# Weight pieces of 576 columns, bonus fills on ScalarE alone, and a list schedule on other durations, in a linear-attention kernel with two gated layers

## Chip, core and metric

The program runs on one core of a Trainium2 chip. The metric is the time of one execution on the device in microseconds (us), as the median of several runs. TensorE (PE) does the matmuls and loads their weights (PEld); VectorE (DVE), ScalarE (ACT) and GpSimd (POOL) do elementwise work; SyncE (SP) issues all DMAs.

## What is computed

A linear recurrence with a decaying state per head, then two feed-forward layers. B, H, S, D are 4, 8, 768, 48; the model width is 384, the two inner widths are 768 and 1536. Cut from the reference:

```python
for t in range(S):
    kt, vt, rt = (k[:, :, t], v[:, :, t], r[:, :, t])
    cur = np.einsum('bhd,bhe->bhde', u[None] * kt, vt)
    y[:, :, t] = np.einsum('bhd,bhde->bhe', rt, state + cur)
    state = w[None, :, :, None] * state + np.einsum('bhd,bhe->bhde', kt, vt)
...
h = np.maximum(np.maximum(x @ w1, x @ w2), x @ w3)      # first layer, float64 weights
x = (h @ w_out).astype(np.float32)
...
g = x @ w_gate                                          # second layer, float64 weights
y = (g * (1.0 / (1.0 + np.exp(-g))) * (x @ w_val) @ w_out).astype(np.float32)
```

r, k, v, w, u are float32. The weights of both layers are float64.

## The kernel before

**Attention.** The 768 steps are cut into six blocks of 128, and a block of one batch entry is a unit (24 units, `n`). A unit scales r and k by powers of the decay (`prep_scores`, L266), multiplies u, k and r for the diagonal (`prep_bonus`, L270 and L271, summed in `bonus`, L280), writes the diagonal for eight heads in eight instructions (`fill`, L286 on DVE or L288 on ACT: the eight are two steps of four), multiplies scores (`scores`, L297), selects them below the diagonal (`select`, L300), and multiplies with v and the state (`apply`, L317 to L326; `outer`, L345).

**Layers.** Every layer product is exact to about float32: operands are split into a high and a low float32r part, and `product` (L384, L385, L386) makes three matmuls of each. The first layer (`m`, `o`) runs for six column blocks `i` between the attention units of the next block; then the second layer (`g`, `oo`) runs for the six blocks. `larger` (L401) and `gate` (L429) on DVE read a layer's PSUM banks; `split_low` (L408) on POOL and `split_lo` (L379) on DVE or POOL make low parts.

**Weights.** Each float64 weight is used six times, but brought in and split once. There are three kinds: `a` (6 tiles of 1152 columns, inner layer 1), `b` (2 tiles, its output), `c` (12 tiles, layer 2). A tile is brought in as pieces of 384 columns, two 32-bit words per weight: 18 + 6 + 36 = 60 pieces. A piece takes ten steps: a fetch (L191, four buffers), a scaling on ACT (`scale`, L196), two or three DVE instructions (`top`: L213, L210, L217), two more (`rest`: L225, L227), two on ACT (`put_hi`, L230; `to_float`, L234), and a product on POOL or DVE (`put_lo`, L238). For `a` and `b` pieces, L210 writes its result into a spare tile (`mid`, a part of `x2[0]`), ahead of L217; for `c` pieces it writes over its own input, behind L217. Blocks of layer 1 need all `a` and `b` tiles in block 0, layer 2 needs all `c` tiles in its block 0; the later blocks need no new weight.

**Order.** `Plan` writes each engine's order ahead of time: a list schedule over steps with a cost per engine, in us, and what each step needs. The order of the matmuls is given by hand (`order`); everything else, and whether DVE, ACT or POOL does a step that may run on several, comes out of the costs. The hardware then runs each engine's list in order, with semaphores.

Of the kernel before, what the change touches and what calls it, by code (L numbers as in the profile page):

```python
# [25 lines left out]
W_LO, W_HI = 0.8, 1.25  # L26

# [125 lines left out]
def rwkv_moe(ctx: ExitStack, tc: tile.TileContext, qk, nat, kn, vn, rn, wcol, wh, uh, wup1, wout1, wup2, out):  # L153
# [31 lines left out]
    nearly = 3 * NF1 + NF1  # L185
    weights, raws, ts = {}, {}, {}
    mid = x2[0].bitcast(U32)[:, 0, 0:384]

    def fetch(k):
        raws[k] = raw_p.tile([128, 384, 2], U32, tag="raw", name=f"raw_{k}", bufs=4)  # L190
        nc.sync.dma_start(out=raws[k].rearrange("p n z -> p (n z)"), in_=jobs[k][2].bitcast(U32))  # L191

    def scale(k):

        ts[k] = raw_p.tile([128, 384], U32, tag="t", name=f"t_{k}")
        nc.scalar.mul(ts[k].bitcast(F32), raws[k][:, :, 1].bitcast(F32), 2.0**-112)  # L196

    def part(k, q):
        key, z, _ = jobs[k]
# [3 lines left out]
        return weights[key][:, q, z]  # L203

    def top(k):

        t, hw = ts[k], raws[k][:, :, 1]

        def middle(o):
            nc.vector.tensor_scalar(out=o, in0=hw, scalar1=0x1FF, scalar2=15,  # L210
                                    op0=ALU.bitwise_and, op1=ALU.logical_shift_left)

        nc.vector.tensor_scalar(out=t, in0=t, scalar1=3, scalar2=0xFFFFF000,  # L213
                                op0=ALU.logical_shift_left, op1=ALU.bitwise_and)
        if k < nearly:
            middle(mid)
        nc.vector.scalar_tensor_tensor(out=t, in0=hw, scalar=0x80000000, in1=t,  # L217
                                       op0=ALU.bitwise_and, op1=ALU.bitwise_or)
        if k >= nearly:
            middle(hw)  # L220

    def rest(k):

        lw, hw = raws[k][:, :, 0], raws[k][:, :, 1]
        nc.vector.scalar_tensor_tensor(out=lw, in0=lw, scalar=17, in1=mid if k < nearly else hw,  # L225
                                       op0=ALU.logical_shift_right, op1=ALU.bitwise_or)
# [192 lines left out]
    def second_phase(_):  # L419
        ph1.close()  # L420
        late["moe2"] = pool(ctx, "moe2", bufs=2)
        late["ps_o"] = pool(ctx, "ps_o", space=PSUM)

# [24 lines left out]
    with tc.manual_schedule():  # L448
# [9 lines left out]
        for k in range(4):  # L458
            fetch(k)
# [85 lines left out]
        def attention_closed(_):  # L545
            att.close()
            late["wp2"] = pool(ctx, "wp2", bufs=4, side="right")
# [43 lines left out]
        both, one = {"dve": 0.6, "pool": 1.25}, {"pool": 1.25}  # L591


        for k, (key, z, _) in enumerate(jobs):
            if k < 4:
                add(("fetch", k), {"none": 0.0}, [], lambda e: None, at=17.5 + 1.1 * k)
            else:
                add(("fetch", k), {"sync": 0.5}, [("lo", k - 4), ("branch",)], lambda e, k=k: fetch(k), lag=3.0)

            room = []  # L600
            if key[0] == "c":
                f = key[1] - 4
                room = [("attention closed",)] if f < 0 else [("m", NB - 1, f, 2)] if f < NF1 else [("o", NB - 1, NK - 1, f - NF1)]
            add(("scale", k), {"act": 0.42}, [("fetch", k)] + ([("hi", k - 2), ("rest", k - 2)] if k > 1 else []),
                lambda e, k=k: scale(k))
            add(("top", k), {"dve": 1.02 if k < nearly else 1.2}, [("scale", k)] + ([("rest", k - 1)] if k else []), lambda e, k=k: top(k))
            add(("rest", k), {"dve": 0.74 if k < nearly else 0.86}, [("top", k)], lambda e, k=k: rest(k))
            add(("hi", k), {"act": 0.42}, [("top", k), ("rest", k)] + room, lambda e, k=k: put_hi(k))
            add(("float", k), {"act": 0.42}, [("rest", k)], lambda e, k=k: to_float(k))
            add(("lo", k), {"pool": 1.14, "dve": 0.5}, [("float", k), ("hi", k)], lambda e, k=k: put_lo(k, engine[e]))  # L610

        def weight(k):
            return [("hi", k), ("lo", k)]
# [3 lines left out]
        for n in range(NB * B):  # L617
# [12 lines left out]
            add(("bonus", n), {"dve": 1.0, "pool": 1.95} if first else {"pool": 1.95}, [("arrived", n)],  # L630
                lambda e, n=n: prep_bonus(n, engine[e]))
            add(("keys", n), {"pool": 0.98}, [("bonus", n)], lambda e, n=n: prep_keys(n), at=9.6)
            pair = {2: 0, 4: 2}.get(n, n - 1 if n > 4 else None)
            add(("s", n), {"pe": 1.25}, [("scaled", n, 0), ("scaled", n, 1)] + bank_free["s", n]
                + ([("select", pair, 0), ("select", pair, 1)] if pair is not None else []), lambda e, n=n: scores(n))
            add(("a0", n), {"dve": 0.5}, [("bonus", n)] + ([("y", two)] if n > 1 else []), lambda e, n=n: bonus(n))
# [167 lines left out]
```

## Time and profile before

| | us |
|---|---|
| three runs | 909.99, 910.24, 912.38 (median 910.24) |
| the profiled execution's own time | 909.89 |
| its span, first to last instruction | 908.2 |
| PE matmuls busy | 865.2 (95%) |
| DVE, ACT, POOL busy | 383.5, 323.4, 365.3 |

Of the page's 40 equal slices of the span (22.7 us each), these rows show the busy tenths:

```profile
PE   7869789999999999999998799999999999999998
DVE  8999973333323322448999941121012012112101
```

How to read it: the share of the whole span hides that the work has stages. PE is at 9 tenths everywhere but in slices 0 to 5 and in 20 to 22; in those slices DVE is at 8 or 9, elsewhere at 1 to 4. Those are the stages in which weights are split: `a` and `b` from about 27 us to 130 us, `c` from about 385 us to 529 us.

### The profile page before, as it was taken

What the parts mean: (1) busy time and instruction counts of PE and PEld (TensorE: products, weight loads), DVE (VectorE), ACT (ScalarE), POOL (GpSimd) and SP (SyncE); (2) the same over time, 40 slices, a digit from 0 to 9 for tenths busy, and PEclk for the clock granted to TensorE, in tenths of its full rate; (3) what the DMA queues carried; (4) which work ended last, traced back from release to release, by engine and by line L of the source; (5) the groups of instructions that cost most, each with busy time, mean ns of one, the idle gap of its engine ahead of it and who ended that gap; (6) DMA issues with size and microseconds to landing.
All of it is one profiled execution on the core that took longest, in us unless ns stands there. A gap on an engine that the chain in (4) does not pass through costs nothing.

```text
span 908.2 us, 12109 instructions
## 1 busy us (share of the span) xinstructions
PE 865.2 (95%) x4754; PEld 703.6 (77%) x4754; DVE 383.5 (42%) x615; ACT 323.4 (36%) x675; POOL 365.3 (40%) x322
## 2 busy tenths in 40 slices
PE   7869789999999999999998799999999999999998
PEld 6647668887887887888876578888888888888886
DVE  8999973333323322448999941121012012112101
ACT  3645644342242333325655542122222113122211
POOL 7575666644546635214444442222221222122221
PEclk8889889999999999999999999999999999999999
DMA  8335432323303302012434300000000000000000
GB/s 264 117 100 184 147 125 67 89 75 94 102 1 93 102 1 93 10 36 70 123 106 122 102 36 1 1 35 1 1 1 35 0 1 35 1 1 35 1 1 35
DMA packets 19323, 55.45 MB, mean 61 GB/s; under 512 B 2400, under 2 KB 3296, under 8 KB 19264
## 3 DMA queue, kind: packets, MB, share of 16 engines
q1 hardware_dynamic: 19264, 54.67, 19.6%
q8 instruction: 37, 0.61, 0.3%
q14 instruction: 22, 0.18, 0.1%
HBM read 48.96 MB, written 4.72 MB: 59 GB/s over the span
## 4 chain that ended last, share of the span: by engine, by line
PE 73%; DVE 17%; issue 3%; ACT 1%; DMA 1%; POOL 0%; DVEq 0%; ACTq 0%; POOLq 0%
PE g L386 9%; PE g L385 9%; PE g L384 9%; PE m L384 7%; PE m L386 6%; PE m L385 6%; PE oo L385 5%; PE oo L386 5%; PE oo L384 5%; DVE t L217 4%; DVE raw L225 3%; DVE t L213 2%; DVE raw L210 2%; PE o L386 2%; PE o L384 2%
## 5 line engine op out<-in xcount | busy, mean ns | idle before, releaser
L408 POOL TENSOR_TENSOR gs<-mm,gs 128x512 fp32r<-128x512 f32 x72 | 93.7, 1302 | 287.0 <-ACT gs L433 286.5
L384 PE MATMUL g<-xhi,w_c 128*128 128x512 f32 x432 | 169.5, 392 | 9.7 <-DVE mm L429 9.3
L429 DVE TENSOR_TENSOR mm<-mm,g 128x512 f32<-128x512 f32 x72 | 49.4, 687 | 300.2 <-PE g L386 299.1
L386 PE MATMUL g<-xhi,w_c 128*128 128x512 f32 x432 | 169.3, 392 | 0.9 <-POOL w_c L238 0.8
L385 PE MATMUL g<-xlo,w_c 128*128 128x512 f32 x432 | 168.7, 391 | 0.0
L384 PE MATMUL m<-xhi,w_a 128*128 128x512 f32 x324 | 133.5, 412 | 4.7 <-DVE h L401 4.7
L386 PE MATMUL m<-xhi,w_a 128*128 128x512 f32 x324 | 129.2, 399 | 2.6 <-DVE w_a L238 2.6
L385 PE MATMUL m<-xlo,w_a 128*128 128x512 f32 x324 | 128.7, 397 | 2.3 <-POOL xlo L379 1.4
L401 DVE TENSOR_TENSOR h<-h,m 128x512 f32<-128x512 f32 x72 | 49.3, 685 | 135.7 <-PE m L386 101.2
L384 PEld LDWEIGHTS g<-xhi,w_c 128*128 128x128 f32 x432 | 81.3, 188 | 29.8 <-DVE mm L429 6.1
L408 POOL TENSOR_TENSOR hs<-h,hs 128x512 fp32r<-128x512 f32 x36 | 54.7, 1519 | 103.3 <-ACT hs L405 103.2
L386 PEld LDWEIGHTS g<-xhi,w_c 128*128 128x128 f32 x432 | 81.4, 188 | 18.8 <-POOL w_c L238 1.9
L385 PEld LDWEIGHTS g<-xlo,w_c 128*128 128x128 f32 x432 | 81.4, 188 | 16.8
L433 ACT CAST gs<-mm 128x512 fp32r<-128x512 f32 x72 | 44.6, 620 | 139.3 <-DVE mm L429 139.3
L426 ACT ACTIVATE mm<-g 128x512 f32<-128x512 f32 x72 | 43.0, 597 | 136.9 <-PE g L386 136.9
L384 PE MATMUL oo<-gs,w_c 128*128 128x512 f32 x216 | 85.8, 397 | 0.7 <-ACT gs L433 0.7
L385 PE MATMUL oo<-gs,w_c 128*128 128x512 f32 x216 | 85.3, 395 | 0.9 <-POOL gs L408 0.9
L386 PE MATMUL oo<-gs,w_c 128*128 128x512 f32 x216 | 85.1, 394 | 0.0
L384 PEld LDWEIGHTS m<-xhi,w_a 128*128 128x128 f32 x324 | 62.2, 192 | 21.1 <-ACT w_b L230 3.3
L386 PEld LDWEIGHTS m<-xhi,w_a 128*128 128x128 f32 x324 | 62.2, 192 | 17.3 <-DVE w_a L238 3.5
L385 PEld LDWEIGHTS m<-xlo,w_a 128*128 128x128 f32 x324 | 62.4, 193 | 14.9 <-POOL xlo L379 1.7
L266 POOL TENSOR_TENSOR qk<-qk,P 112x512 f32<-112x512 f32 x43 | 57.0, 1343 | 26.9 <-DMA qk<-in_qk 26.9
(107 smaller groups left out, 1243.7 us busy)
## 6 DMA issues: line engine op xcount, KB each, us to landing
raw<-in_wup SPq DMA_DIRECT2D x54, 384.0 KB, 3.2
nat<-in_nat SPq DMA_DIRECT2D x22, 576.0 KB, 5.1
qk<-in_qk SPq DMA_DIRECT2D x24, 448.0 KB, 4.4
out<-ob SPq DMA_DIRECT2D x18, 256.0 KB, 2.1
raw<-in_wout SPq DMA_DIRECT2D x6, 384.0 KB, 3.3
xr<-xr SPq DMA_DIRECT2D x10, 96.0 KB, 3.0
kv<-in_nat SPq DMA_DIRECT2D x4, 192.0 KB, 9.5
r<-in_nat SPq DMA_DIRECT2D x2, 192.0 KB, 8.2
```

What stands on the lines that cost most here:

```text
L210: nc.vector.tensor_scalar(out=o, in0=hw, scalar1=0x1FF, scalar2=15, op0=ALU.bitwise_and, op1=ALU.logical_shift_left)
L217: nc.vector.scalar_tensor_tensor(out=t, in0=hw, scalar=0x80000000, in1=t, op0=ALU.bitwise_and, op1=ALU.bitwise_or)
L225: nc.vector.scalar_tensor_tensor(out=lw, in0=lw, scalar=17, in1=mid if k < nearly else hw, op0=ALU.logical_shift_right, op1=ALU.bitwise_or)
L266: eng.tensor_tensor(out=a, in0=a, in1=P[0:112], op=ALU.mult)
L384: nc.tensor.matmul(p, wh_, xh, start=first, stop=False)
L385: nc.tensor.matmul(p, wh_, xl, start=False, stop=False)
L386: nc.tensor.matmul(p, wl_, xh, start=False, stop=last)
L401: nc.vector.tensor_tensor(out=hs[i, f], in0=hs[i, f], in1=banks["m", i, f, j], op=ALU.max)
L408: eng.tensor_tensor(out=g[:, 1], in0=m, in1=g[:, 0].bitcast(F32), op=ALU.subtract)
L426: nc.scalar.activation(out=hs[i, f], in_=banks["g", i, f, 0], func=AF.Silu)
L429: nc.vector.tensor_tensor(out=hs[i, f], in0=hs[i, f], in1=banks["g", i, f, 1], op=ALU.mult)
L433: nc.scalar.copy(hsplit[i, f][:, 0], hs[i, f])
```

## The change

Tiles `a` and `c` are brought in as two pieces of 576 columns (a piece may now end inside a 384-column part), `b` in pieces of 384 as before: 12 + 6 + 24 = 42 pieces, with three buffers. The spare tile `mid` goes: in every piece the second word's middle bits are written in place, behind the instruction that reads it. `rest` is split in `rest` and `power`. The bonus fills of the first four units may no longer run on DVE. Three tiles of `c` (not four) wait in the pool that takes the attention's room, one more in a new pool. Costs in the plan are others throughout; two are shown.

```diff
-    jobs = ([(("a", f), z, wup1[f, :, z * 384:(z + 1) * 384]) for f in range(NF1) for z in range(3)]
-            + [(("b", g), z, wout1[3 * g + z]) for g in range(NF1 // 3) for z in range(3)]
-            + [(("c", f), z, wup2[f, :, z * 384:(z + 1) * 384]) for f in range(NF2) for z in range(3)])
+    jobs = ([(("a", f), z, HALF, wup1[f, :, z:z + HALF]) for f in range(NF1) for z in (0, HALF)]
+            + [(("b", g), 384 * z, 384, wout1[3 * g + z]) for g in range(NF1 // 3) for z in range(3)]
+            + [(("c", f), z, HALF, wup2[f, :, z:z + HALF]) for f in range(NF2) for z in (0, HALF)])
...
-        raws[k] = raw_p.tile([128, 384, 2], U32, tag="raw", name=f"raw_{k}", bufs=4)
+        raws[k] = raw_p.tile([128, HALF, 2], U32, tag="raw", name=f"raw_{k}", bufs=3)
...
-            where = late["wp2"] if key[0] == "c" and key[1] < 4 else wpool
+            where = late["wp3" if key[1] == NF2 - 1 else "wp2"] if key[0] == "c" and not 3 <= key[1] < NF2 - 1 else wpool
...
         nc.vector.tensor_scalar(out=t, in0=t, scalar1=3, scalar2=0xFFFFF000,
                                 op0=ALU.logical_shift_left, op1=ALU.bitwise_and)
-        if k < nearly:
-            middle(mid)
         nc.vector.scalar_tensor_tensor(out=t, in0=hw, scalar=0x80000000, in1=t,
                                        op0=ALU.bitwise_and, op1=ALU.bitwise_or)
-        if k >= nearly:
-            middle(hw)
 
     def rest(k):
...
-        nc.vector.scalar_tensor_tensor(out=lw, in0=lw, scalar=17, in1=mid if k < nearly else hw,
+        lw, hw = words(k)
+        nc.vector.tensor_scalar(out=hw, in0=hw, scalar1=0x1FF, scalar2=15,
+                                op0=ALU.bitwise_and, op1=ALU.logical_shift_left)
+        nc.vector.scalar_tensor_tensor(out=lw, in0=lw, scalar=17, in1=hw,
                                        op0=ALU.logical_shift_right, op1=ALU.bitwise_or)
...
+    def power(k):
+
+        nc.vector.tensor_scalar(out=words(k)[1], in0=ts[k], scalar1=0xFF800000, scalar2=None, op0=ALU.bitwise_and)
...
-            add(("lo", k), {"pool": 1.14, "dve": 0.5}, [("float", k), ("hi", k)], lambda e, k=k: put_lo(k, engine[e]))
+            add(("lo", k), {"pool": 1.7 * wide_, "dve": 0.9 * wide_}, [("float", k), ("power", k), ("hi", k)],
...
-                add(("fill", n, x), {"act": 1.2, "dve": 0.75} if first else {"act": 1.2}, [("a0", n)],
+                add(("fill", n, x), {"act": 1.6}, [("a0", n)],
```

What it moves, at three places. In the changed file DVE's five weight instructions are L213, L215, L221, L223 and L228, the product is L239, the gate L431.

DVE, first layer, one piece of an `a` tile with what stands around it (`t` is the scaled word, `raw` the two words of a piece, `x_0` the spare tile, `h` a block of layer 1). Before:

```order
L213 TENSOR_SCALAR t_708<-t_708 128x384
L210 TENSOR_SCALAR x_0_88<-raw_665 128x384
L217 SCALAR_TENSOR_TENSOR t_708<-raw_665,t_708 128x384
L225 SCALAR_TENSOR_TENSOR raw_665<-raw_665,x_0_88 128x384
L227 TENSOR_SCALAR raw_665<-t_708 128x384
L401 TENSOR_TENSOR h_0_705<-h_0_705,m_0_1_692 128x512
```

and now:

```order
L213 TENSOR_SCALAR t_678<-t_678 128x576
L215 SCALAR_TENSOR_TENSOR t_678<-raw_644,t_678 128x576
L221 TENSOR_SCALAR raw_644<-raw_644 128x576
L223 SCALAR_TENSOR_TENSOR raw_644<-raw_644 128x576
L228 TENSOR_SCALAR raw_644<-t_678 128x576
L402 TENSOR_TENSOR h_0_700<-h_0_700,m_0_1_686 128x512
L239 TENSOR_TENSOR w_a_680<-raw_644 128x576
```

Each of the first four instructions is now followed at once by one that needs it; before, an independent one stood between. Of the 18 products of `a` tiles, DVE did six and POOL twelve; of the 12 now, DVE does two and POOL ten.

DVE, second layer, from the third gate on (`mm` is the gated block). Before:

```order
L429 TENSOR_TENSOR mm_2_4135<-mm_2_4135,g_2_1_4122 128x512
L213 TENSOR_SCALAR t_4158<-t_4158 128x384
L217 SCALAR_TENSOR_TENSOR t_4158<-raw_4113,t_4158 128x384
L210 TENSOR_SCALAR raw_4113<-raw_4113 128x384
L225 SCALAR_TENSOR_TENSOR raw_4113<-raw_4113 128x384
L227 TENSOR_SCALAR raw_4113<-t_4158 128x384
L213 TENSOR_SCALAR t_4181<-t_4181 128x384
```

(a second piece follows, before the fourth gate) and now:

```order
L431 TENSOR_TENSOR mm_2_4016<-mm_2_4016,g_2_1_4001 128x512
L228 TENSOR_SCALAR raw_3974<-t_4014 128x576
L213 TENSOR_SCALAR t_4054<-t_4054 128x576
L215 SCALAR_TENSOR_TENSOR t_4054<-raw_4012,t_4054 128x576
L221 TENSOR_SCALAR raw_4012<-raw_4012 128x576
L223 SCALAR_TENSOR_TENSOR raw_4012<-raw_4012 128x576
L228 TENSOR_SCALAR raw_4012<-t_4054 128x576
L431 TENSOR_TENSOR mm_3_4070<-mm_3_4070,g_3_1_4059 128x512
```

Between the first gate and the end of the last piece, DVE has 22 pieces of 384 before and 15 of 576 now, and eleven gates in both. The chain of five inside a `c` piece is the same.

ACT, the fills of the first units (`am` takes the diagonal, `y` and `u` are matmul results). Before:

```order
L288 ACTIVATE am_222<-aeye,a_0_221 128x128 x4
L288 ACTIVATE am_270<-aeye,a_1_269 128x128 x4
L334 COPY xr_291<-y_254 128x3x128
L357 COPY st_131<-u_282 112x192
L288 ACTIVATE am_315<-aeye,a_2_314 128x128 x4
```

and now:

```order
L289 ACTIVATE am_206<-aeye,a_0_205 128x128 x8
L289 ACTIVATE am_253<-aeye,a_1_252 128x128 x8
L335 COPY xr_301<-y_261 128x3x128
L289 ACTIVATE am_299<-aeye,a_2_298 128x128 x8
```

DVE's twelve fills of units 0 to 2 went to ACT. DVE takes over the bonus products of units 0 and 3, and POOL two of the five scalings that DVE had.

## Rows read from the trace of the kernel before

**Rows 1.** Busy time by stretch: us, PE, PEld, DVE, ACT, POOL busy (instructions), PEclk, DMA, GB/s

```profile
30.00:130.00 100.00, 80.32 (x546) 62.31 (x546) 92.37 (x158) 57.50 (x132) 61.30 (x50) 0.86 0.48 153
442.83:537.00 94.17, 82.06 (x325) 63.27 (x324) 84.46 (x141) 53.25 (x106) 44.20 (x39) 0.95 0.33 95
451.10:528.80 77.70, 67.12 (x270) 51.66 (x269) 72.72 (x122) 42.57 (x86) 35.95 (x32) 0.96 0.35 102
537.00:610.45 73.45, 73.45 (x325) 60.81 (x324) 11.36 (x16) 17.47 (x29) 16.70 (x13) 1.00 0.03 11
```

**Rows 2.** Waits of PE over the whole span: us in total, times, longest us

```profile
PE g L384 <- DVE mm L429: 9.3, 6, 2.4
PE y L326 <- DVE am L300: 8.1, 3, 4.3
PE m L384 <- DVE h L401: 4.7, 3, 3.0
```

**Rows 3.** Stretches, instructions on tile raw alone: us, DVE, ACT, POOL busy

```profile
30.00:130.00 100.00, 64.48 (x102) 25.05 (x47) 19.11 (x17) 0.86 0.48 153
451.10:528.80 77.70, 57.34 (x89) 22.86 (x44) 22.70 (x22) 0.96 0.35 102
```

**Rows 4.** The same stretches, L213 alone: us, DVE busy

```profile
30.00:130.00 100.00, 12.81 (x24) 0.86 0.48 153
451.10:528.80 77.70, 11.48 (x22) 0.96 0.35 102
```

**Rows 5.** First stretch, L238 alone (the product): us, DVE busy, POOL busy

```profile
30.00:130.00 100.00, 6.12 (x6) 19.11 (x17) 0.86 0.48 153
```

**Rows 6.** Groups by shape in 451.1 to 528.8: busy us, mean ns, idle before

```profile
L429 DVE TENSOR_TENSOR mm<-mm,g 128x512 f32<-128x512 f32 x11 | 7.5, 678 | 0.0
L408 POOL TENSOR_TENSOR gs<-mm,gs 128x512 fp32r<-128x512 f32 x10 | 13.5, 1346 | 18.4 <-ACT gs L433 17.9 <-DVE t L213 0.4
```

**Rows 7.** One line's instructions, 384 columns: duration ns min/median/max, first and last start

```profile
L213 DVE TENSOR_SCALAR t<-t x60: 340/353/1472, 30.0 to 524.7; 128x384 uint32<-128x384 uint32 x60
L217 DVE SCALAR_TENSOR_TENSOR t<-raw,t x60: 544/559/1686, 30.5 to 525.6; 128x384 uint32<-128x384 uint32 x60
```

**Rows 8.** The same view, pairs of like instructions at 512 and 384 columns

```profile
L379 DVE TENSOR_TENSOR xlo<-x,xhi x12: 678/696/1821, 435.7 to 828.6; 128x512 fp32r<-128x512 f32 x12
L270 DVE TENSOR_TENSOR r<-kv,r x1: 544/544/544, 23.4 to 23.4; 128x384 f32<-128x384 f32 x1
L408 POOL TENSOR_TENSOR gs<-mm,gs x72: 1278/1287/1721, 452.9 to 899.8; 128x512 fp32r<-128x512 f32 x72
L270 POOL TENSOR_TENSOR nat<-nat x22: 995/1021/1466, 8.8 to 357.6; 128x384 f32<-128x384 f32 x22
```

**Rows 9.** Timeline of DVE, an `a` piece and a `c` piece: start us, us

```profile
41.50 0.55 DVE L217 SCALAR_TENSOR_TENSOR t<-raw,t 128x384 uint32<-128x384 uint32 x1
41.97 0.55 DVE L225 SCALAR_TENSOR_TENSOR raw<-raw,x 128x384 uint32<-128x384 uint32 x1
...
448.65 0.56 DVE L217 SCALAR_TENSOR_TENSOR t<-raw,t 128x384 uint32<-128x384 uint32 x1
449.31 0.88 DVE L210 TENSOR_SCALAR raw<-raw 128x384 uint32<-128x384 uint32 x1
```

**Rows 10.** Timeline of POOL at 33.47 us

```profile
33.47 3.01 POOL L238 TENSOR_TENSOR w_a<-raw 128x384 fp32r<-128x384 f32 x1 [6.56 <-ACT raw L234]
```

**Rows 11.** Timeline of DVE, the first unit's fills and selects

```profile
12.42 3.74 DVE L286 TENSOR_SCALAR am<-aeye,a 128x128 f32<-128x128 f32 x4
16.26 1.34 DVE L300 COPY_PREDICATED am<-mask,s 128x512 f32<-128x512 uint8 x2
```

**Rows 12.** Groups in 8 to 30 us: ACT's fills

```profile
L288 ACT ACTIVATE am<-aeye,a 128x128 f32<-128x128 f32 x17 | 5.4, 390 | 12.9 <-DVE a L280 12.9
```

**Rows 13.** DMA issues: KB each, median us to landing

```profile
raw<-in_wup SPq DMA_DIRECT2D x54, 384.0 KB, 3.2
nat<-in_nat SPq DMA_DIRECT2D x22, 576.0 KB, 5.1
```

More of the change, by code (lines that the diff above doesn't have):

```diff
@@ L234, in to_float @@
         nc.scalar.mul(lw.bitcast(F32), lw, 2.0**-35)
     def put_lo(k, eng):
-        raw = raws.pop(k)
-        eng.tensor_tensor(
-            out=part(k, 1), in0=raw[:, :, 1].bitcast(F32), in1=raw[:, :, 0].bitcast(F32), op=ALU.mult)
+        lw, hw = (x.bitcast(F32) for x in words(k))
+        eng.tensor_tensor(out=part(k, 1), in0=hw, in1=lw, op=ALU.mult)
+        del raws[k], ts[k]
     inp, a0s, ams, sc, ys, ups, xr = {}, {}, {}, {}, {}, {}, {}
@@ L422, in second_phase @@
         late["ps_o"] = pool(ctx, "ps_o", space=PSUM)
+        late["wp3"] = pool(ctx, "wp3", side="right")
     def silu(i, f):
@@ L457, in rwkv_moe @@
             load_unit(n)
-        for k in range(4):
+        for k in range(3):
             fetch(k)
@@ L590, in rwkv_moe @@
         add = plan.add
[L591 to L596, printed above, removed]
+        both, one = {"dve": 0.9, "pool": 1.4}, {"pool": 1.45}
+        TOP, REST, POWER = 1.35, 1.35, 0.5
+        for k, (key, z, n, _) in enumerate(jobs):
+            if k < 3:
+                add(("fetch", k), {"none": 0.0}, [], lambda e: None, at=17.5 + 1.7 * k)
@@ L597, in rwkv_moe @@
             else:
-                add(("fetch", k), {"sync": 0.5}, [("lo", k - 4), ("branch",)], lambda e, k=k: fetch(k), lag=3.0)
+                add(("fetch", k), {"sync": 0.5}, [("lo", k - 3), ("branch",)], lambda e, k=k: fetch(k), lag=3.5)
             room = []
             if key[0] == "c":
[L602 to L605, printed above, removed]
@@ L612, in weight @@
-        def weight(k):
-            return [("hi", k), ("lo", k)]
+                f = key[1] - 3
+                room = [("attention closed",) if f < 0 else ("m", NB - 1, f, 2) if f < NF1
+                        else ("o", NB - 1, NK - 1, f - NF1) if f < NF1 + 2 else ("second phase",)]
+            wide_ = n / HALF
+            cast = {"act": 0.2 + 0.48 * wide_}
+            add(("scale", k), cast, [("fetch", k)] + ([("hi", k - 2), ("power", k - 2)] if k > 1 else []), lambda e, k=k: scale(k))
@@ L616, in rwkv_moe, with weight @@
+        def weight(kind, f, j):
+            if kind == "b":
+                return [("lo", 2 * NF1 + f)]
+            k = 2 * f + (nearly if kind == "c" else 0)
+            return [("lo", k + q) for q in ((0,), (0, 1), (1,))[j]]
         arrive = ((5.5, 7.3), (9.0, 10.6), (11.9, 13.5), (14.8, 16.4))
@@ L642, in rwkv_moe @@
+            add(("y", n), {"pe": 2.6 if first else 2.15}, [("select", n, 0), ("select", n, 1)]
                 + ([("row", n - 1)] if n else []) + ([] if first else [("update", n - B)]), lambda e, n=n: apply(n))
-            add(("row", n), {"act": 0.5}, [("y", n)] + ([("xlo", i - 1, k) for k in range(NK)] if i else []),
+            add(("row", n), {"act": 0.6}, [("y", n)] + ([("xlo", i - 1, k) for k in range(NK)] if i else []),
                 lambda e, n=n: evacuate(n))
-            add(("u", n), {"pe": 0.02 if last else 0.5}, [("y", n), ("keys", n)] + bank_free["u", n]
+            add(("u", n), {"pe": 0.02 if last else 0.6}, [("y", n), ("keys", n)] + bank_free["u", n]
```

86 lines of the change are left out of this document (43 added, 43 removed).

## The prediction, made before the changed kernel had run

> **What bounds the kernel now.** I read the slices first, then the stretches, then PE's waits, then DVE inside the two stages that matter. Over the span PE is busy 95%, but by stretch it is not. In 30 to 130 us PE is busy 80.3 of 100 us at a granted clock of 0.86, and DVE 92.4; in 442.8 to 537.0, the first block of layer 2, PE needs 94.17 us for 325 matmuls, and in the next stretch, for as many of the same, 73.45 us at full clock [rows 1]. So the second weight stage alone loses 94.17 - 73.45 = 20.7 us, and that is the most that any faster splitting of `c` can give there. What PE waits for is a DVE result in all its three largest waits: the gate, the select, the maximum [rows 2]. Those instructions are short; they stand behind weight pieces in DVE's queue. From 130 us to 443 us and from 537 us on PE runs without a gap, so what is won or lost in either stage moves the end by as much.
>
> **A piece on DVE now, second stage.** From the first gate at 451.1 us to the end of the last piece at 528.8 us DVE is busy 72.72 of 77.70 us [rows 1]: it is the bound. Of that 57.34 + 11.48 = 68.8 us are the 22 pieces [rows 3, 4] and 7.5 us eleven gates [rows 6]. With the 4.98 us of idle time this makes 81.3, 3.6 more than the stretch, since neighbouring rows overlap at their ends. So a piece costs 68.8 / 22 = 3.13 of rows, +0.23 idle, -0.16 overlap: 3.20 us. Undisturbed, its five instructions take 3 x 0.353 + 2 x 0.559 = 2.18 us (the one-input form three times, the two-input form twice) [rows 7]. With 0.07 net for gaps that leaves 0.95 us per piece, 20.9 us in all, in which DVE's instructions are stretched; POOL is busy 35.95 us there [rows 1], and a like instruction's longest row is three to four times its median on either engine [rows 7, 10]. I take these 20.9 us as waits of the two engines for each other.
>
> **A wider piece.** Two-input DVE instructions take 678 ns at 512 columns and 544 at 384 [rows 8]: 1.05 ns a column, so +0.20 us for 192 more. One-input ones are not shown at two widths. Their cost is between nothing and the same 0.20; L213 at 353 ns against L217 at 559, with the same fixed part of 559 - 384 x 1.05 = 156 ns, has half the slope, so I take +0.10. A piece of 576 costs 2 x 0.20 + 3 x 0.10 = 0.70 us more, undisturbed. On POOL 1287 against 1021 ns [rows 8] gives 2.08 ns a column: +0.40 us for a product.
>
> **Second stage, after.** 15 pieces of 2.18 + 0.07 + 0.70 = 2.95 make 44.3 us, 22 of 2.25 made 49.5: 5.2 us less. The mutual waits have two bounds. If they go by POOL's time, 15 products of 22.70 / 22 + 0.40 = 1.43 us [rows 3] and 13.5 us of low parts [rows 6] are 35.0 against 36.2 us, and 20.9 us shrink by 0.7. If they go by the number of POOL instructions, 25 against 32, they shrink by 4.6. So the stage gains 5.9 to 9.8 us; I take the middle, **-7.8**.
>
> **First stage.** Here the edit cuts both ways. Removed: six pieces, and four of DVE's six products. Added: columns, and a chain. Today an independent instruction stands between those that need each other, and each starts 41.50 + 0.55 - 41.97 = 0.08 us before the last one's row ends; in a `c` piece, a chain, the next one starts 449.31 - 449.21 = 0.10 us after it [rows 9]. So a piece now costs 2.18 - 5 x 0.08 = 1.78 us undisturbed, and a chained one 2.25. 18 x 2.25 + 12 x 0.70 = 48.9 against 24 x 1.78 = 42.7: +6.2 us. Products on DVE: 6.12 us for six [rows 5], after it two of 1.22: -3.7 us. The rest of the 64.48 + 12.81 - 6.12 = 71.2 us that DVE spends on 24 pieces [rows 3 to 5], less 0.16 of overlap each, is 2.81 - 1.78 = 1.03 us a piece, 24.7 us of mutual waits. By POOL's time they grow: 16 products, ten of them of 1.52 us, are 2.8 us more on 61.3 [rows 1, 5], +1.1. By the number of DVE instructions that meet them, 92 against 126, they shrink by 6.7. Sum: +3.6 to -4.2. I take **+1.5**, nearer the upper end, because of the row at 33.47 us: a POOL product, 1.12 us in the mean, took 3.01 us behind an unbroken run of DVE instructions and got in when the run broke [rows 10]. A chain breaks the run after every instruction, so POOL gets in more often and DVE waits more often.
>
> What the Trainium skill says speaks against this term: in "VectorE: DVE Perf Modes", section "The DRAIN you can't avoid", eight copies took the same time with a semaphore after each as with one after the last. By that a chain is free, and the sum would be 8.5 us lower. Rows 9 disagree (overlap in one form, a gap in the other), so the sum goes by the rows.
>
> **Head.** The first unit's four DVE fills take 3.74 us and the selects start at 16.26 [rows 11]. Eight on ACT, at 5.4 / 17 = 0.32 us each [rows 12], end about 2.6 us after 12.4: the selects could start 1.2 us earlier. Unit 1 may gain the same; nothing may come of it if the bonus products that DVE takes over, or the scalings that POOL takes over, are late in their turn. Between 0 and -2.4 I take **-0.8**. ACT does these fills on its idle time (12.9 us ahead of the 17 there); if it were not free, the selects would be what waits.
>
> **What costs nothing, and its cover.** ACT's three steps per piece are off the path (42.6 of 77.7 us busy). Fetches: three buffers instead of four, 576 KB instead of 384. A transfer of 576 KB lands in 5.1 us, one of 384 in 3.2 [rows 13]. A buffer's round is 5.1, two ACT steps of about 0.52 + 0.16 [rows 3], 2.95 + 1.4 of DVE, 1.43 of POOL: 12.2 us, a third of it 4.1 per piece, against (44.3 + 20 + 7.5) / 15 = 4.8 us at which DVE takes pieces. Covered by 0.7 us; before, it was 8.5 / 4 = 2.1 against 3.2. If landings took over 7.2 us, each further one would cost a third of it per piece, 5 us in all for the 15.
>
> **Sum**: -7.8 + 1.5 - 0.8 = -7.1 us against the profiled execution's 909.89, so 902.8; the median of the runs is 0.35 above that execution, so **903.1 us**.
>
> **Rivals.**
> - *Waits go by time, not by number* (13%): both stages at their upper ends, or one-input instructions at the full slope. -5.9 + 3.6 - 0.8 = -3.1; with the slope's 0.10 more on some instructions about -1.5: 908.5. For it: a wait lasts as long as the instruction waited for, and POOL's total time hardly falls. Against it: some DVE instructions meet no POOL one at all, and fewer ends mean fewer meetings.
> - *Slower* (9%): in the first stage POOL becomes the bound. It takes over four products, 4 x 1.52 = 6.1 us, in a fixed order among scalings and low parts that PE waits for. If these are not hidden, the stage costs 6.2 - 3.7 + 1.1 + 6.1 = +9.7, the second gains its lower 5.9, the head nothing: +3.8, so 914.0. It decides once the first stage loses more than the 8.6 us that the rest gives. For it: POOL is busy 61.3 of 100 us already, and its order is fixed. Against it: its 38.7 us of idle time.
> - *A free chain* (8%): the first stage gains 7.0 instead of losing 1.5, so 894.6 us. This is the page's rule. For it nothing here but that the `a` chain might be filled with other steps' instructions; the order shows few.
> - That the edit does not do what it says is excluded by the order: 22 pieces become 15.
>
> **How the numbers follow.** A measurement of this kernel can tell about 0.3%, 2.7 us, from no change. The forecast (70%) spans 897 to 907.5: all terms' better ends together would give 893.8, and are unlikely together. Faster: 70 + 8 = 78%; the same: 13%; slower: 9%. The range from 897 to 909.5 holds the forecast and the first rival and leaves out the other two, 17%.
>
> **What would show it.** Right: from first gate to last piece about 70 us instead of 77.7; PE's wait for the gate below 5 us; the five weight instructions' rows at about 0.45 and 0.76 us undisturbed; first block of layer 2 at about 86 us; its start within 3 us of 442.8. Wrong: that start later by over 5 us with POOL as PE's releaser in the first stage; ACT's scaling waiting for a fetch in the second; one-input rows at 0.55.

## The result: 1.0% faster, and the profile after

Four runs of the changed kernel took 900.78 to 902.76 us, median **901.88**; the kernel before, beside it, had a median of 910.81. The ratio is 0.9899, 95% interval 0.9881 to 0.9918: faster by 1.0%, 1.2 us below the 903.1 that was forecast and inside its range. The profiled execution took 900.78 us, its span is 899.0.

The sum was right; its terms were not, so the close hit is partly luck. From the two traces, by the start of the first matmul of each kind (us):

| | before | after | difference | forecast |
|---|---|---|---|---|
| first matmul of layer 1 (`m`) | 36.22 | 33.26 | -3.0 | -0.8 |
| from there to the first of layer 2 (`g`) | 406.61 | 409.82 | +3.2 | +1.5 |
| first block of layer 2 | 94.17 | 84.62 | -9.6 | -7.8 |
| from its second block to PE's end | 367.37 | 367.36 | 0.0 | 0 |
| sum | | | -9.3 | -7.1 |

The busy time by stretch in the changed kernel, with the columns of [rows 1] (the first stage, the first block of layer 2, from its first gate to the end of its last piece, the block after):

```profile
30.00:130.00 100.00, 78.23 (x503) 59.30 (x499) 95.42 (x118) 51.94 (x105) 64.85 (x51) 0.88 0.49 154
443.08:527.70 84.62, 77.46 (x325) 61.33 (x324) 74.78 (x94) 48.73 (x77) 40.67 (x30) 0.98 0.32 99
448.40:519.00 70.60, 64.97 (x271) 50.98 (x269) 65.65 (x83) 39.68 (x64) 34.92 (x25) 0.98 0.36 110
527.70:601.15 73.45, 73.45 (x326) 60.81 (x325) 11.38 (x16) 17.47 (x29) 16.70 (x13) 1.00 0.03 11
```

The third line answers to 77.70 us of [rows 1]; about 70 had been forecast. The block of the second line is 11.2 us above the 73.45 of the block after it, where it was 20.7 above. Of the 9.6 us that the block lost, 5.0 are idle time of PE and 4.6 its busy time (82.06 to 77.46 us for as many matmuls, at a mean granted clock of 0.98 of full speed instead of 0.95); no run separates the two. In the first line DVE is busy 95.4 us instead of 92.4, for 40 instructions fewer.

PE's waits over the whole span: us in total, times, longest:

```profile
PE m L385 <- DVE h L402: 5.7, 3, 2.9
PE y L327 <- DVE am L301: 5.5, 6, 2.4
PE g L387 <- POOL w_c L239: 5.3, 4, 2.4
```

The wait for the gate, 9.3 us in [rows 2], is gone from the top (1.5 us, once). In its place PE waits for a weight's low part from POOL: the last step of a piece is now late by itself, not what stood ahead of a gate.

The weight instructions one by one, as in [rows 7] (ns, least, median, most):

```profile
L213 DVE TENSOR_SCALAR t<-t x42: 349/455/1410, 28.0 to 514.0; 128x576 uint32<-128x576 uint32 x36, 128x384 uint32<-128x384 uint32 x6
L215 DVE SCALAR_TENSOR_TENSOR t<-raw,t x42: 557/1458/3150, 28.5 to 515.4; 128x576 uint32<-128x576 uint32 x36, 128x384 uint32<-128x384 uint32 x6
L223 DVE SCALAR_TENSOR_TENSOR raw<-raw x42: 558/760/1710, 29.8 to 517.7; 128x576 uint32<-128x576 uint32 x36, 128x384 uint32<-128x384 uint32 x6
L239 POOL TENSOR_TENSOR w_c<-raw x24: 1147/1150/1749, 398.3 to 519.3; 128x576 fp32r<-128x576 f32 x24
```

455 and 760 ns are the undisturbed durations at 576 columns; 0.45 and 0.76 had been forecast. L215 is the odd one: its median is nearly twice L223's, for the same operation and size. It is the one that is held up most.

DVE's busy time on the same lines in the first stage and from the first gate on, `raw` and then L213 (us, DVE, in the first two rows also ACT and POOL busy):

```profile
30.00:130.00 100.00, 69.05 (x72) 22.02 (x34) 18.35 (x16) 0.88 0.49 154
448.40:519.00 70.60, 49.77 (x58) 20.08 (x29) 20.18 (x15) 0.98 0.36 110
30.00:130.00 100.00, 11.71 (x17) 0.88 0.49 154
448.40:519.00 70.60, 11.24 (x14) 0.98 0.36 110
```

Second stage: 61.0 us for 72 instructions (43 one-input, 29 two-input). Undisturbed they are 43 x 0.455 + 29 x 0.760 = 41.6, so they are stretched by 19.4 us. Before it was 68.8 for 111 [rows 3, 4], 67 x 0.353 + 44 x 0.559 = 48.2 undisturbed, 20.6 stretched. Of the 7.8 us that the rows lost, 6.6 are undisturbed time and 1.2 are mutual waits.

The head, on ACT and on DVE, where [rows 11] had fills of 3.74 us on DVE and the selects at 16.26:

```profile
10.38 2.45 ACT L289 ACTIVATE am<-aeye,a 128x128 f32<-128x128 f32 x8
```
```profile
13.20 1.35 DVE L301 COPY_PREDICATED am<-mask,s 128x512 f32<-128x512 uint8 x2 [1.84 <-PE s L298]
```

The selects start 3.1 us earlier, and no longer wait for a fill but for the scores. Those came later, at 11.9 us instead of 10.1: one of the first unit's two scalings stands on POOL now, the first of these two, and ends at 10.8 us, where both were done on DVE at 9.35 before. From 9.7 us up to the scores PE worked on the tile `spare`; whether they could have started sooner is not shown.

```profile
9.22 3.27 POOL L267 TENSOR_TENSOR qk<-qk,P 112x512 f32<-112x512 f32 x2
```

The same row, by a window that ends between the two:

```profile
9.22 1.59 POOL L267 TENSOR_TENSOR qk<-qk,P 112x512 f32<-112x512 f32 x1
```

### The profile page after: what moved, and what is told of

The parts are those of the page before. It is cut to its first block, busy times and chain, and to the rows that moved or that the text cites. A ratio compares the mean times of both kernels' runs of the same rounds, so it can differ in the third digit from the quotient of the medians.

```text
span 899.0 us, 11874 instructions
## 1 busy us (share of the span) xinstructions
PE 858.1 (95%) x4774; PEld 698.3 (78%) x4774; DVE 378.8 (42%) x511; ACT 322.4 (36%) x633; POOL 363.7 (40%) x306
## 3 DMA queue, kind: packets, MB, share of 16 engines
q1 hardware_dynamic: 16672, 54.67, 19.4%
## 4 chain that ended last, share of the span: by engine, by line
PE 76%; DVE 18%; issue 3%; ACT 1%; POOL 1%; DMA 1%; DVEq 0%; POOLq 0%; SPq 0%; ACTq 0%
PE g L387 9%; PE g L385 9%; PE g L386 9%; PE m L385 8%; PE m L387 7%; PE m L386 7%; DVE t L215 5%; PE oo L385 5%; PE oo L386 5%; PE oo L387 5%; DVE raw L221 3%; DVE raw L223 3%; DVE t L213 3%; PE s L298 2%; PE o L387 2%
## 5 line engine op out<-in xcount | busy, mean ns | idle before, releaser
L409 POOL TENSOR_TENSOR gs<-mm,gs 128x512 fp32r<-128x512 f32 x72 | 94.8, 1317 | 277.7 <-ACT gs L435 273.2
L431 DVE TENSOR_TENSOR mm<-mm,g 128x512 f32<-128x512 f32 x72 | 49.5, 687 | 301.3 <-PE g L387 301.3
L409 POOL TENSOR_TENSOR hs<-h,hs 128x512 fp32r<-128x512 f32 x36 | 54.2, 1507 | 90.9 <-ACT hs L406 90.8
L386 PE MATMUL oo<-gs,w_c 128*128 128x512 f32 x216 | 84.6, 392 | 0.1
L385 PE MATMUL oo<-gs,w_c 128*128 128x512 f32 x216 | 84.5, 391 | 0.0
L387 PE MATMUL oo<-gs,w_c 128*128 128x512 f32 x216 | 84.3, 390 | 0.0
L267 POOL TENSOR_TENSOR qk<-qk,P 112x512 f32<-112x512 f32 x45 | 63.2, 1413 | 23.3 <-DMA qk<-in_qk 23.3
```

Source lines behind the costliest of these rows:

```text
L267: eng.tensor_tensor(out=a, in0=a, in1=P[0:112], op=ALU.mult)
L385: nc.tensor.matmul(p, wh_, xh, start=first, stop=False)
L386: nc.tensor.matmul(p, wh_, xl, start=False, stop=False)
L387: nc.tensor.matmul(p, wl_, xh, start=False, stop=last)
L409: eng.tensor_tensor(out=g[:, 1], in0=m, in1=g[:, 0].bitcast(F32), op=ALU.subtract)
L431: nc.vector.tensor_tensor(out=hs[i, f], in0=hs[i, f], in1=banks["g", i, f, 1], op=ALU.mult)
```

## The experiments

All times are medians beside runs of the kernel before on the same chip (910.3 to 911.2 us). Of each trace the table has the start of the first scores, of the first `m`, the time from there to the first `g` (first stage: from 130 us on PE runs without a gap) and the length of the first block of layer 2 (second stage). A trace is one execution, and twelve executions of one kernel, that of the third row, took 904.46 to 910.65 us; so differences of the columns need not add up to those of the medians.

| | time | interval of the ratio | scores | first `m` | to `g` | block |
|---|---|---|---|---|---|---|
| before | 910.4 | | 10.1 | 36.2 | 406.6 | 94.2 |
| fills alone | 908.3 | 0.9963 to 0.9993 | 10.8 | 31.5 | 410.1 | 94.2 |
| 384, spare tile | 908.0 | 0.9964 to 0.9989 | 13.3 | 33.8 | 407.1 | 91.7 |
| 576, spare tile | 898.7 | 0.9842 to 0.9880 | 13.6 | 35.6 | 405.9 | 84.6 |
| the change | 901.9 | 0.9881 to 0.9918 | 11.9 | 33.3 | 409.8 | 84.6 |
| 384, no spare tile | 916.7 | 1.0050 to 1.0087 | 13.3 | 36.2 | 414.9 | 92.4 |
| 576, two spare tiles | 893.6 | 0.9804 to 0.9837 | 13.1 | 35.6 | 404.4 | 80.5 |
| change, products in halves | 897.0 | 0.9834 to 0.9874 | 13.1 | 33.1 | 407.0 | 83.7 |
| change, old head costs | 897.7 | 0.9844 to 0.9874 | 9.9 | 34.1 | 405.9 | 84.7 |
| two spare tiles, products in halves | 891.2 | 0.9775 to 0.9812 | 14.2 | 34.1 | 405.6 | 78.1 |
| two spare tiles, old head costs | 889.2 | 0.9752 to 0.9785 | 10.3 | 34.1 | 403.7 | 79.9 |
| the last + products on DVE | 888.8 | 0.9755 to 0.9786 | 10.5 | 34.6 | 402.5 | 77.5 |
| + low parts in halves as well | 891.9 | 0.9766 to 0.9809 | 10.2 | 34.7 | 406.1 | 80.9 |
| instead: products, low parts in halves | 885.5 | 0.9706 to 0.9744 | 10.7 | 34.4 | 400.8 | 77.4 |

The first five rows are a path from the kernel before to the change. Its steps are the fills; the new durations, together with the split of `rest`; the width, with three buffers instead of four; and the chain. The rows with two spare tiles are the change without its chain, some with one more edit.

**The fills alone.**

```diff
-                add(("fill", n, x), {"act": 1.2, "dve": 0.75} if first else {"act": 1.2}, [("a0", n)],
+                add(("fill", n, x), {"act": 1.2}, [("a0", n)],
```

> The kernel before with one edit: the bonus fills of the first four units may run on ScalarE alone. By the prediction's term for the head: -0.8 us (0 to -2.4), so about 910.0 where the kernel before has 910.8, and the first matmul of layer 1 starts about 0.8 us earlier than 36.22 us. Rival, that the fills alone make the whole of what the changed kernel gained ahead of layer 1: first matmul of layer 1 at about 33.3 us (2.96 us earlier), time about 907.9. Both: the two weight stages as long as before (99.1 and 94.2 us).

908.26 us, 2.1 us faster. Layer 1 begins 4.7 us earlier, more than either text said, but the stage behind it is 3.5 us longer: DVE, which was busy 92.4 of 100 us there [rows 1], still has as many pieces to do. The head and the first stage are not two terms that add up.

**Narrow pieces with the spare tile, all else as changed.**

```diff
-    jobs = ([(("a", f), z, HALF, wup1[f, :, z:z + HALF]) for f in range(NF1) for z in (0, HALF)]
+    jobs = ([(("a", f), z, 384, wup1[f, :, z:z + 384]) for f in range(NF1) for z in (0, 384, 768)]
...
+    mid = x2[0].bitcast(U32).rearrange("p k t -> p (k t)")[:, 0:HALF]
...
+        if k < nearly:
+            nc.vector.tensor_scalar(out=mid[:, 0:jobs[k][2]], in0=hw, scalar1=0x1FF, scalar2=15,
+                                    op0=ALU.bitwise_and, op1=ALU.logical_shift_left)
```

> The changed kernel, with pieces of 384 columns and four buffers, and with the spare tile for the a and b pieces, as before; what is left of the change is the fills, the split of the middle step in two, and the new durations. By the prediction, which gave the new durations no term: as the kernel before but for the head, so 0 to -2.4 us, about 910.0. Rival, that the new order is worth something by itself: the first gate, which stood behind pieces, comes 5.3 us after layer 2 begins, as in the changed kernel, instead of 8.3, and about 3 us are gained in the first block of layer 2; time about 905 to 907.

908.01 us: beside the fills alone the new durations are worth nothing that can be measured. Yet the rival was right about the place. The first gate comes 6.6 us after layer 2 begins (8.3 before, 5.3 after), and the block is 2.5 us shorter. The head is longer, with the first scores at 13.3 us and the first `m` 2.3 us later than with the fills alone; the first stage is 3.0 us shorter. In sum that trace gained 3.2 us, but it is of an execution of 905.46 us, 2.6 below the median; where the median loses the gain again is not shown.

**Wide pieces with the spare tile.** The change with the spare tile's lines from above, for `a` and `b` pieces.

> The changed kernel, with the spare tile again for the a and b pieces, now 576 columns, so that an independent instruction stands between those that need each other; nothing else differs but what the plan makes of it. A free chain (the rival of the prediction): no change, 901.9. A chain that costs its gaps alone (four of 0.035 + 0.08 us in 18 pieces, 8.3 us of DVE): the first stage, 102.3 us from the first matmul of layer 1 to that of its second block, 3 to 8 us shorter, time 894 to 899, and DVE's instructions are stretched as before, 0.37 us each in the mean beyond their undisturbed time. A chain whose every gap lets POOL in ahead of DVE: the stretch falls to the 0.20 us of the kernel before as well, 90 x 0.17 = 15 us more of DVE's time, and the first stage is shorter by more than 8 us, as far as PE lets it.

898.72 us, 3.2 us less than the change. The first stage is 3.9 us shorter, behind a head that is 2.4 longer; as with the fills, the two may trade. Where the head is the same (the first `m` at 34.1 us in both runs with the old head costs, below), the chain is worth 2.2 us of the first stage. DVE in an `a` piece of the change (start us, us), each instruction starting 0.03 to 0.04 us after the last one's row has ended:

```profile
40.89 0.46 DVE L213 TENSOR_SCALAR t<-t 128x576 uint32<-128x576 uint32 x1
41.38 1.74 DVE L215 SCALAR_TENSOR_TENSOR t<-raw,t 128x576 uint32<-128x576 uint32 x1
```

and with the spare tile, each starting 0.08 us before:

```profile
42.44 0.45 DVE L214 TENSOR_SCALAR t<-t 128x576 uint32<-128x576 uint32 x1
42.81 0.45 DVE L217 TENSOR_SCALAR x<-raw 128x576 uint32<-128x576 uint32 x1
43.18 1.70 DVE L219 SCALAR_TENSOR_TENSOR t<-raw,t 128x576 uint32<-128x576 uint32 x1
```

A chain is not free. Its gaps are four of about 0.115 us in a piece, 8.3 us in 18 pieces, and less than half of that reaches the end. It costs no more than its gaps at this width: the time by which DVE's instructions are stretched (table below) stays at 31 to 32 us. That a gap lets POOL in, on which the forecast's +1.5 rested, falls. In an unbroken run the third instruction is held up as long (1.70 us).

**A second spare tile, for `c`.**

```diff
             late["wp2"] = pool(ctx, "wp2", bufs=3, side="right")
+            mids[True] = late["wp2"].tile([128, HALF], U32, name="mid", bufs=1)
```

> As the run before it, and a second spare tile, in the room that attention leaves, for the c pieces too. In the second stage a chain costs 3 x 0.115 + 0.19 = 0.53 us per piece by its gaps, 7.7 us for 14.4 pieces after the first gate. A free chain: no change there. Gaps alone: the first block of layer 2, 84.6 us now, takes about 77. Gaps that let POOL in: the mean stretch of a DVE weight instruction there, 0.24 us (28.4 us for 120), falls towards 0.14, so 12 us more of DVE's time, and the block comes down to what PE needs, 73.5 us: 11 us less than the changed kernel in this stage alone. Time of the kernel: 901.9 less what the spare tile gives in the first stage, and less 0, 7.5 or 11.

893.61 us. Its first block of layer 2, with the columns of [rows 1]:

```profile
440.05:520.53 80.48, 75.39 (x326) 60.27 (x324) 70.88 (x93) 47.94 (x77) 42.81 (x29) 1.00 0.33 104
```

80.5 us, 4.1 less than the change has, and 3.9 us of DVE's busy time less. About half of the 7.7 us of gaps reaches the end; the stretch does not fall here either. With the old head costs in both, the two spare tiles give 8.6 us (897.73 to 889.16), here 8.3.

**Narrow pieces in a chain:** all of the change but the width.

> The changed kernel with pieces of 384 columns and four buffers, without a spare tile: all of the change but the width. The prediction's prices (a chain costs 0.47 us of a piece, 24 pieces; 7 more pieces after the first gate at 2.25, 15 at 0.70 less): first stage 24 x 0.47 = 11.3 us longer than with narrow pieces and a spare tile (99.6), second stage 7.0 longer than the changed kernel's 84.6; time about 915. If a broken chain costs its gaps alone, measured at 3.9 us for 18 pieces, it costs 5.2 for 24: first stage 104.8, second 91.6, time about 912. If the width is worth more where the chain is broken: over 915.

916.67 us, slower than before by 0.7%. The same stretch here:

```profile
451.11:543.46 92.35, 78.21 (x325) 59.27 (x324) 85.31 (x144) 54.47 (x106) 41.98 (x38) 1.00 0.34 99
```
The width is worth 14.8 us to the change, and carries it: without it, the rest of the change loses 6 us. With the spare tile it is worth 9.3 (908.01 to 898.72), so the third text's number came, but not its reason. The chain costs the first stage 7.8 us in 24 pieces, 0.32 us each, where the forecast had 0.47 and the gaps alone, as the text took them from the run before, 0.22. The difference is not explained: 2.0 us more of stretch (table below) are part of it, and the trace with the spare tile is of an execution 2.6 us below its median. In the second stage, with a chain in both, 384 against 576 columns is 92.4 against 84.6.

**Products in halves**, first in the change, then with both spare tiles.

```diff
-        eng.tensor_tensor(out=part(k, 1), in0=hw, in1=lw, op=ALU.mult)
+        o, n = part(k, 1), jobs[k][2] // 2
+        for c in (slice(0, n), slice(n, 2 * n)):
+            eng.tensor_tensor(out=o[:, c], in0=hw[:, c], in1=lw[:, c], op=ALU.mult)
```

> The changed kernel, with every product of a piece written as two instructions of half the columns, on whichever engine does it. In the changed kernel DVE's weight instructions are stretched by 60.6 us in both stages, and POOL's elementwise rows there are 95 and sum to 128 us, the products 39 of them with 48.8 us. From 1148 ns at 576 columns and 827 at 384, a product costs about 0.19 us more in two halves, 7.6 us of POOL's time for 40. If DVE waits by POOL's time (60.6 of 128, 0.47): 3.6 us more of DVE's time, kernel at 902 to 906. If it waits by the number of POOL's instructions (95 become 134): 25 us more, 912 to 927. If a DVE instruction waits for the rest of the one POOL instruction that it meets, so that a shorter one holds it up less and the second half is not met again: the products' share of the wait, about 23 us, falls towards a half, 890 to 897.

> The run with both spare tiles (893.6 us), and the products in halves. By POOL's time: 0 to 4 us slower, 894 to 898. By the number of instructions: over 903. By the length of the instruction that is met: 882 to 889; the unbroken runs of DVE leave POOL's second half to wait, so it could be worth less here than in the kernel with chains.

897.04 us, 4.8 faster, and 891.17 us, 2.4 faster: both between the texts' cases. The intervals of the second and of its kernel with whole products overlap (0.9775 to 0.9812, 0.9804 to 0.9837), so it is not clear of noise alone. In the change, half a product takes (ns, least, median, most):

```profile
L241 POOL TENSOR_TENSOR w_c<-raw x48: 661/837/1261, 395.3 to 514.9; 128x288 fp32r<-128x288 f32 x48
```

That waits go by the number of POOL's instructions is excluded; POOL has 40 more and DVE waits 5.4 us less. That they go by POOL's time is too: its rows in the two stages sum to 146.9 us instead of 128.0. Worked out from the rows, the change has 74 DVE weight instructions that are over 0.1 us longer than undisturbed, 0.81 us in the mean, and with halves there are 94, of 0.58: more meetings, and shorter ones. A shorter instruction holds DVE up less, by far less than half.

**The head's costs**, with both spare tiles and then in the change alone.

```diff
-                add(("scaled", n, q), both if first else one, [("load", n)],
+                add(("scaled", n, q), {"dve": 0.6, "pool": 1.25} if first else one, [("load", n)],
...
-            add(("bonus", n), {"dve": 1.2, "pool": 2.15} if first else {"pool": 2.15}, [("arrived", n)],
+            add(("bonus", n), {"dve": 1.0, "pool": 1.95} if first else {"pool": 2.15}, [("arrived", n)],
```

(and the sums, fills and selects of all units at their old costs).

> The run with both spare tiles (893.6 us), and the costs of the first four units' steps (scalings, bonus products, their sum, fills, selects) as in the kernel before, so that DVE does the first unit's scalings and POOL its bonus product again. If the changed order of the head costs time, as the first scores (13.1 us in that run, 10.8 in the one with the fills alone) and the first matmul of layer 1 (35.6 against 31.5) suggest: 2 to 4 us faster, 890 to 892. If the first stage, bound by DVE, takes back what the head gives, as it did with the fills alone (head 4.7 us shorter, first stage 3.5 longer): within 1.5 us of 893.6.

> The changed kernel, with the costs of the first four units' steps alone as in the kernel before; the fills stay on ScalarE, the chain and the width as in the change. If the new order of the head cost the change what it cost the kernel with both spare tiles (4.5 us): about 897.4. If the head's gain is lost in the first stage where the chain makes DVE's work longer: 900 to 902.

889.16 us, 4.5 faster, and 897.73, 4.2 faster than the change. Here the new costs made a worse order. The gain is not in the head as far as the first `m` (34.1 us instead of 33.3 in the change) but in the first stage, 3.9 us shorter; which of the five costs gives it is not shown. In the trace of the second both scalings of the first unit stand on DVE again:

```profile
7.20 2.14 DVE L267 TENSOR_TENSOR qk<-qk,P 112x512 f32<-112x512 f32 x2
```

They are done at 9.34 us; in the change the one on POOL ended at 10.8. The first scores start at 9.9.

**POOL's work moved or cut**, on the kernel of 889.2 us: products on DVE alone, products and POOL's low parts (L409) in halves, products on DVE and low parts in halves.

```diff
-            add(("lo", k), {"pool": 1.7 * wide_, "dve": 0.9 * wide_}, [("float", k), ("power", k), ("hi", k)],
+            add(("lo", k), {"dve": 0.9 * wide_}, [("float", k), ("power", k), ("hi", k)],
...
-        eng.tensor_tensor(out=g[:, 1], in0=m, in1=g[:, 0].bitcast(F32), op=ALU.subtract)
+        for c in (slice(0, NT // 2), slice(NT // 2, NT)):
+            eng.tensor_tensor(out=g[:, 1, c], in0=m[:, c], in1=g[:, 0, c].bitcast(F32), op=ALU.subtract)
```

> The run with both spare tiles and the old head costs (889.2 us), with every product of a piece on VectorE. DVE does 35 more in both stages, at 0.745 to 0.76 us undisturbed 26 us; POOL loses about 39 rows, 50 of its 130 us. If DVE's waits are a fixed share of POOL's time (61 of 130 us, 0.47): they shrink by 23 us, so no gain and no loss, 887 to 893. If DVE waits about 30 us in each stage whatever POOL does there, as all runs so far show (27 to 34): 26 us more on the engine that bounds both stages, 900 to 915. If PE's waits for POOL's products (5.3 us, 4 times, in the first block of layer 2) go as well: 880 to 886.

> The run with both spare tiles and the old head costs (889.2 us), with products and POOL's low parts of h and gs (512 columns, 1.29 us) in halves. If a shorter POOL instruction holds DVE up less, as with the products alone in the kernel with chains (4.8 us faster) and less with both spare tiles (2.4): 883 to 887. If the fixed part of each more POOL instruction, 0.19 us, outweighs that: 889 to 893; in the later blocks PE has no gap that this could lengthen.

> The run with every product on VectorE (888.8 us), and POOL's low parts of h and gs in halves. If halves help wherever POOL and DVE meet: faster by 1 to 3 us, 886 to 888, still not below the 885.5 of the run with products on POOL in halves. If the gain of that run came from the products' halves alone: 888 to 890.

888.80, **885.49** and 891.93 us. The first is the sharpest look at the mutual waits. Groups from the first gate on (x, busy us, mean ns, idle before and its releaser), with both spare tiles:

```profile
L231 DVE TENSOR_SCALAR raw<-t 128x576 uint32<-128x576 uint32 x15 | 9.6, 639 | 0.0
L214 DVE TENSOR_SCALAR t<-t 128x576 uint32<-128x576 uint32 x14 | 9.2, 658 | 4.1 <-ACT t L202 4.1
L202 ACT ACTIVATE t<-raw 128x576 f32<-128x576 f32 x14 | 10.2, 730 | 6.6 <-DMA raw<-in_wup 6.6
```

and with the products on DVE:

```profile
L242 DVE TENSOR_TENSOR w_c<-raw 128x576 fp32r<-128x576 f32 x15 | 14.3, 951 | 1.3 <-ACT raw L238 1.1
L231 DVE TENSOR_SCALAR raw<-t 128x576 uint32<-128x576 uint32 x16 | 7.2, 451 | 0.0
L214 DVE TENSOR_SCALAR t<-t 128x576 uint32<-128x576 uint32 x15 | 6.8, 452 | 0.3 <-ACT t L202 0.2
L202 ACT ACTIVATE t<-raw 128x576 f32<-128x576 f32 x15 | 11.0, 734 | 15.2 <-DMA raw<-in_wup 12.7 <-DVE mm L434 2.3
```

With POOL's products gone, the one-input rows are at their undisturbed 451 ns. In both stages together DVE does 39 us more (42 products of 40.8 us in sum, instead of two of 1.5), and its waits fall by 33 us (30.3 and 30.7 to 18.8 and 9.2 in the table below). The first case of the text had the time right, but its 23 us of waits were too few. ACT now waits 12.7 us for fetches, but DVE waits for ACT's scaling only 0.2 us, so that costs nothing there; with both spare tiles and products on POOL, DVE stood 4.1 us for that step, which had waited 6.6 us for fetches (L214 and L202 in the first of the two views). A fourth buffer was not tried. Halves (885.49) are the best version of all. The last run, a combination of the two, was a miss: 3.1 us slower by the medians, though the intervals overlap. In its trace PE waited 4.4 us for POOL's low parts in the second stage, 2.7 with them whole; but that execution is 3.3 us above the median, and its mean granted clock is 0.94 from 130 to 160 us, where it is 1.00 with whole low parts. Why halving them helps beside products on POOL and not without them stays open.

**DVE's stretch in all this**, worked out from the rows: for each weight instruction its duration less the undisturbed one (0.353 and 0.555 us at 384 columns, 0.455 and 0.760 at 576), summed from the first `m` to 3 us before the second block's (first stage), and from 385 to 530 us (second); beside it the number of these instructions, and POOL's elementwise rows, which hold POOL's own waits too.

| | DVE, first | POOL, first | DVE, second | POOL, second |
|---|---|---|---|---|
| before | 23.9 us in 106 | 61.8 us in 51 | 31.8 in 180 | 59.1 in 53 |
| fills alone | 23.9 in 106 | 64.1 in 53 | 31.4 in 179 | 60.9 in 54 |
| 384, spare tile | 31.6 in 106 | 70.7 in 57 | 30.5 in 178 | 61.6 in 55 |
| 576, spare tile | 31.4 in 80 | 71.8 in 54 | 28.4 in 119 | 61.4 in 44 |
| the change | 32.2 in 82 | 66.7 in 51 | 28.4 in 120 | 61.3 in 44 |
| 384, no spare tile | 33.6 in 108 | 65.5 in 57 | 29.5 in 173 | 60.4 in 53 |
| change, old head costs | 28.7 in 78 | 65.0 in 49 | 28.5 in 116 | 61.7 in 44 |
| two spare tiles | 29.7 in 80 | 73.1 in 52 | 30.3 in 116 | 65.1 in 45 |
| two spare tiles, old head costs | 30.3 in 76 | 67.8 in 51 | 30.7 in 111 | 62.7 in 46 |
| change, products in halves | 28.3 in 81 | 73.1 in 66 | 26.9 in 117 | 73.8 in 69 |
| products on DVE | 18.8 in 77 | 60.0 in 39 | 9.2 in 110 | 34.3 in 23 |

That these are waits for POOL is seen row by row: in every run each weight instruction that is over 0.1 us longer than undisturbed overlaps a row of POOL (74 of 74 in the change), while of the others most do not (22 of 128 do). DVE's number of instructions (180 against 116) hardly matters; nor does the chain. Taking the products off POOL is what cut the waits most, and halving them cut a little. POOL's sum by itself predicts little: about 65 us of it stand beside 23.9, 28.7 and 33.6 us of waits in the first stage.

## Why the prediction was right, and where its steps were not

- **Second stage, -7.8; measured -9.6.** Undisturbed time was right: a piece at 2.88 us, measured 3 x 0.455 + 2 x 0.760 = 2.885. (POOL's product was priced at 0.40 us more; least rows of 827 and 1147 ns make it 0.32.) The mutual waits shrank by 1.2 us, near the end "by POOL's time" (0.7), not by the 2.65 of the middle. The width as a whole, with durations and chain alike, gave 91.7 to 84.6, **-7.0**. What the forecast lacked is the other -2.5, which came with the new durations and the split of `rest`: the first gate comes 1.7 us sooner after the start of layer 2 (8.3 to 6.6), and I had costed the order at nothing.
- **First stage, +1.5; measured +3.2.** Two terms were mis-sized, in opposite directions. The chain was priced at its gaps, 18 x 0.47 = 8.5 us. The gaps are there in the rows, but 3.9 us reached the end beside the same kernel with the spare tile, and 2.2 with equal heads. The mutual waits I took to lie between +1.1 and -6.7; in the table they grew by 8.3 us, from 23.9 to 32.2. The spare tile hardly changes them (31.4), nor does the width (31.6 at 384): they rose in the step with the new durations and the split of `rest`. POOL has more to do there (70.7 us instead of 61.8 with narrow pieces), but that this is why is not shown, and the old head costs alone take 3.5 us back. The stage still ended only 3.2 us later: the chain cost less, and DVE's idle time there, 7.6 us of 100, fell to 4.6.
- **Head, -0.8; measured -3.0 to layer 1.** I counted the first unit's four fills and perhaps the second's. DVE made twelve before, 8.2 us in sum:

```profile
L286 DVE TENSOR_SCALAR am<-aeye,a 128x128 f32<-128x128 f32 x12 | 8.2, 744 | 0.1
```

With these alone gone, layer 1 began 4.7 us earlier. But the step behind it failed twice. What the head gives is taken back in the stage bound by DVE (3.5 of 4.7 us with the fills alone), and the new costs of the attention's steps lose 4.2 us of the whole. POOL's takeover of scalings, which I named as a reason that nothing may come of it, is one of the things that they bring.
- **What cancelled.** Head and first stage together: +0.7 forecast, +0.2 measured. Within the first stage a chain priced too high hid waits priced too low. The second stage's order alone is more than the 1.2 us by which the total was off. That the sum came so close is in part luck.
- **Fetches.** 576 KB landed in 3.7 us (median), not the 5.1 of [rows 13], so the cover was wider than 0.7 us; ACT's scaling waited 2.0 us for fetches from the first gate on, which I had set as a sign of failure. It is small, and DVE idled 2.2 us for that step in the same stretch:

```profile
L201 ACT ACTIVATE t<-raw 128x576 f32<-128x576 f32 x14 | 10.2, 727 | 2.2 <-DMA raw<-in_wup 2.0
```

- **Rivals.** "By time, not by number" was near in the second stage (0.7 us against 1.2), but not in the first (1.1 against 8.3), and the halves speak against it; its 908.5 (its own -1.5 makes 908.7) had no gain from the order. "POOL the bound of the first stage" is excluded: POOL was busy 64.9 of 100 us, and PE's waits there for POOL are 3.6 us (for `xlo` and `w_b`). "A free chain" is excluded by the runs with spare tiles (3.2 and 5.1 us). In the Trainium skill's "VectorE: DVE Perf Modes", section "The DRAIN you can't avoid", eight copies cost the same with a semaphore after each as with one after the last. That does not carry over to these chains: an instruction that needs the one before starts 0.03 to 0.11 us after its end, and one that does not 0.08 us before it.

## What to carry to other kernels

Where two engines hold each other up, shorten the instructions of the one that isn't the bound; moving its work to the other cuts the waits, but here the work ate the gain (889.2 to 888.8 us). Counting the instructions of the bound predicts nothing. Wider tiles pay by their fixed parts, and paid more where each instruction waits for the last (14.8 against 9.3 us); a spare tile that breaks such a chain pays again. Costs in a list schedule are an edit of their own: run them apart from the rest, since a gain of several us in one stage can hide a loss of as much in another.

## What was not expected of the hardware

- DVE's waits for POOL came to 24 to 34 us per stage in all runs with products on POOL, for 76 to 180 DVE instructions and 44 to 92 POOL ones; only with POOL's products gone did they fall below, to 18.8 and 9.2 us.
- Of a piece's two-input instructions the first is held up most: in the second stage its stretch is 0.52 us in the mean against 0.07 for the other with the chain, and 0.50 against 0.28 without it (two spare tiles). Why was not tried.
- Two POOL instructions of half the size made the change 4.8 us faster, though least rows of 661 and 1147 ns make two halves 0.18 us longer than one whole.
